# Converting a weight slot's blocks in one instruction per step

## The chip, the cores and the metric

The kernel runs on one core of a Trainium2 chip. The metric is the time of one execution on the device in microseconds (us); the median of several runs is compared. A core has a matrix engine (TensorE, PE in the profile; its weight loads are shown as PEld), a vector engine (VectorE, DVE), a scalar engine for activation functions, copies and casts (ScalarE, ACT), a general one (GpSimd, POOL) and a queue engine (SyncE, SP), which issues all the transfers of this kernel. Each engine works through its own instructions in a fixed order and waits for the others by semaphores.

## The reference

Local and global attention, then two feed-forward layers over the 2304 tokens, 512 wide, in float32:

```python
# attention: 4 batches, 8 heads, 512 local tokens (window +-32) and 32 global ones, head 64
out_g = softmax(q_g @ [k_g, k_l]^T / 8) @ [v_g, v_l]
out_l = softmax([q_l @ k_g^T, masked q_l @ k_l^T] / 8) @ [v_g, v_l]
x = concat(out_g, out_l)                       # 2304 x 512
# layer 1: w_gate, w_val 512 x 1536, w_out 1536 x 512
xn = x / sqrt(mean(x * x) + 1e-6) * rms_g
x = (silu(xn @ w_gate) * (xn @ w_val)) @ w_out
# layer 2: w_in 512 x 2048, w_out 2048 x 512
h = relu(x @ w_in)
out = (s * h * h + b) @ w_out
```

The weights come as float64, as raw 64-bit words.

## The kernel before

**Tiling.** The tokens are split into five groups: three of 512 columns, two of 320. For each group the kernel runs through 28 weight slots: 12 of phase 1 (layer 1, one slot per 128 hidden units: three blocks of 128 x 512, for gate, value and output) and 16 of phase 2 (layer 2: two blocks, input and output). Each float32 product is made of three matmuls with a high and a low part of the operands (`mm3`, lines 584 to 588). A slot's first matmuls go to a PSUM bank (tag `m`, two banks), are turned into `h` on ACT and DVE, and a slot later `emit_second` accumulates `h` times the output block in `acc`. Between the matmuls of a group, `tick` puts in the steps of the attention for the next group and of the build of its `X`, with lags worked out from PE's time.

**Weights.** During group 0 the raw words of the slots come from memory and are converted. `load_raw` (line 146) fetches one block of 512 KB into a tile `wr` (four tiles). `conv(n, j)` (line 156) converts one block: ACT takes the absolute value of the high words (L166), DVE clamps (L167), shifts (L168), puts in the sign (L169) and the low bits (L170, into a tile `wf`), ACT casts to the high part and DVE subtracts for the low part (`hl`, lines 137 to 139). Then the next raw block is asked for, and after a slot's last block the converted slot is written back to memory (`wsc`, L177). The tiles are `cv` (two), `wf` (three) and the weight tiles `w` of three blocks (six, `W_BUFS`). The conversion of slot `n + 2` is emitted in slot `n`, in pieces: after the gate's matmuls, after `h`, after `emit_second`. In groups 1 to 4 `load_w` (line 179) fetches a converted slot, emitted four slots ahead (`W_LEAD`), when a `w` tile is free.

**Start.** `start` (line 450 on) computes the attention of group 0 in eight units (`S_`, `N_`, `T_`, `V_`), builds the first `X` in two halves of 256 columns (`build_steps`: squares, `norm`, `scale`) and converts slots 0 and 1. Its inputs `s_w` lie in four of the six `w` tiles until they are used.

**Order.** The instructions are emitted by the code above and then ordered for each engine, before the run, by a planner that goes by priority and by its own estimate of when operands are ready; `hp(o)` lifts the priority by `o` places. In the run each queue keeps that order. An instruction that finds its tile or its operand not ready holds up all behind it on its engine, on SP too.

Of the kernel before, what the change touches and what calls it, by code (L numbers as in the profile page):

```python
# [9 lines left out]
F32 = mybir.dt.float32  # L10
F32R = mybir.dt.float32r
I32 = mybir.dt.int32
I64 = mybir.dt.int64
AF = mybir.ActivationFunctionType
ALU = mybir.AluOpType
# [36 lines left out]
GN = [sum(seg_len(s) for s in g) for g in GROUPS]  # L52
GO = [sum(GN[:i]) for i in range(len(GN))]
NMAX = max(GN)
W_BUFS = 6
W_LEAD = 4


@with_exitstack
def attn_moe_kernel(ctx: ExitStack, tc: tile.TileContext, s0, q, k, v, w1, w2, cst, out):  # L60
    nc = tc.nc
    pool = lambda name, bufs=1, **kw: ctx.enter_context(tc.tile_pool(name=name, bufs=bufs, **kw))
    cp = pool("cst")
    wr_p = pool("wr", 4)
    cv_p = pool("cv", 2)
    wf_p = pool("wf", 3)
    w_p = pool("w", W_BUFS)
    act_p = pool("act", 2)
    tmp_p = pool("tmp", 2)
# [76 lines left out]
    def load_raw():  # L146
        if nload[0] >= len(blocks):
            return
        n, j = blocks[nload[0]]
        nload[0] += 1  # L150
        ph, _, f = slots[n]
        t = wr_p.tile([128, 512], I64, tag="wr", name="wr")
        nc.sync.dma_start(out=t, in_=(w1 if ph == 1 else w2)[f, :, j])
        wraw[n, j] = t

    def conv(n, j):
        if n >= n0 or j >= nblk(n):
            return
        r = wraw.pop((n, j)).bitcast(I32).rearrange("p (n t) -> p n t", t=2)
        lo, hi = r[:, :, 0], r[:, :, 1]  # L160
        g = cv_p.tile([128, 512], F32, tag="cv", name="cv")
        t = g.bitcast(I32)
        wf = wf_p.tile([128, 512], F32, tag="wf", name="wf")
        w = w_tile(n)
        with hp(20):
            A.activation(out=g, in_=hi.bitcast(F32), func=AF.Abs)  # L166
            V.tensor_scalar(out=g, in0=g, scalar1=W_LO, scalar2=W_HI, op0=ALU.max, op1=ALU.min)  # L167
            V.tensor_scalar(out=t, in0=t, scalar1=3, scalar2=0x3FFFFFFF, op0=ALU.logical_shift_left, op1=ALU.bitwise_and)  # L168
            V.scalar_tensor_tensor(out=t, in0=hi, scalar=-0x40000000, in1=t, op0=ALU.bitwise_and, op1=ALU.bitwise_or)  # L169
            V.scalar_tensor_tensor(out=wf.bitcast(I32), in0=lo, scalar=29, in1=t,  # L170
                                   op0=ALU.logical_shift_right, op1=ALU.bitwise_or)
        with hp(40):
            hl(w[:, j, 0], w[:, j, 1], wf, "A")
        load_raw()
        if j == nblk(n) - 1:
            wsc[n] = dr_p.tile([128, nblk(n), 2, 512], F32, name=f"wsc{n}")
            nc.sync.dma_start(out=wsc[n], in_=w[:, 0:nblk(n)].bitcast(F32))  # L177

    def load_w(n):
        if n < n0 or n >= len(slots):  # L180
# [264 lines left out]
    def start():  # L445
        rw = []
        spare = []

        def ld(i):
            if not spare:  # L450
                t = w_p.tile([128, 2, 1216], F32, tag="w", name="s_w")
                spare.extend((t[:, 0], t[:, 1]))
            t = spare.pop(0)
            nc.sync.dma_start(out=t, in_=s0[i])
            rw.append((t[:, 0:256], t[:, 256:704].rearrange("p (c n) -> p c n", c=2),
                       t[:, 704:1216].rearrange("p (c t h d) -> p c t h d", c=2, t=2, h=2)))

        ld(0)
        nc.sync.dma_start(out=ct, in_=cst)
        ld(1)  # L460
        load_raw()
        ld(2)
        load_raw()
        ld(3)
        load_raw()
        ld(4)
        load_raw()
        for i in (5, 6, 7):
            ld(i)
        A.preload_act_table_set("natural_log_exp_and_others")  # L470
        G.memset(ones, 1.0)
        G.memset(zeros, 0.0)
        G.memset(epsc, EPS)
        G.memset(qf, 0.0)
        G.memset(pg[:, 0:64], 0.0)
        bk = one_bank()
        for _ in range(4):
            PE.matmul(bk[:, 0:128], lhsT=ones, rhs=ones)

        P = [pm[:, 0:2], pm[:, 2:4]]  # L480
        P += [act_p.tile([128, 2, 2, KW], F32, tag="h", name="s_p") for _ in range(2)]
        st = [cp.tile([128, 3, 4], F32, name=f"sst{i}") for i in range(8)]
        bn = [0]

        def nb():
            bn[0] += 1
            return banks("acc0" if bn[0] % 2 else "at")

        def S_(i):
            qr, kr, vr = rw[i]  # L490
            hf, pp = i // 4, P[i % 4]
            bk = nb()
            mms = []
            for c in range(2):
                for h in range(2):
                    x = slice(64 * h, 64 * h + 64)
                    mms.append(PE.matmul(bk[:, h, c * KW:(c + 1) * KW], lhsT=qr[x, 128 * c:128 * c + 128], rhs=kr[x, c]))
            in_turn(mms)
            for h in range(2):
                for c in range(2):  # L500
                    n = 2 * c + h
                    neg_scaled(pp[:, c, h], bk[:, h, c * KW:(c + 1) * KW], cmask(2 * hf + c), st[i][:, 0, n:n + 1])
                for c in range(2):
                    n = 2 * c + h
                    A.activation(out=pp[:, c, h], in_=pp[:, c, h], func=AF.Exp, scale=-1.0,
                                 bias=st[i][:, 0, n:n + 1], accum_out=st[i][:, 1, n:n + 1])

        def N_(i):
            V.tensor_scalar(out=st[i][:, 2], in0=st[i][:, 1], scalar1=1e-9, scalar2=None, op0=ALU.add)
            V.reciprocal(out=st[i][:, 2], in_=st[i][:, 2])  # L510
            for n in range(4):
                x = P[i % 4][:, n // 2, n % 2]
                norm_eng(x, x, st[i][:, 2, n:n + 1], "V")

        pts = {}

        def T_(i):
            bk = nb()
            mms = []
            for c in range(2):  # L520
                for h in range(2):
                    mms.append(PE.transpose(bk[:, c, 256 * h:256 * h + 128], P[i % 4][:, c, h, 0:128], ident))
                    mms.append(PE.transpose(bk[:, c, 256 * h + 128:256 * h + 256], P[i % 4][:, c, h, 96:KW], ident))
            in_turn(mms)
            t = pt_p.tile([128, 2, 2, 2, 128], F32, tag="pt", name="s_pt")
            A.copy(out=t.rearrange("p c h t n -> p c (h t n)"), in_=bk)
            pts[i] = t

        def V_(i):
            bk = one_bank()  # L530
            vr = rw[i][2]
            mms = []
            for c in range(2):
                for ty in (1, 0):
                    for h in range(2):
                        mms.append(PE.matmul(bk[64 * h:64 * h + 64, 128 * c:128 * c + 128], lhsT=vr[:, c, ty, h],
                                             rhs=pts[i][:, c, h, ty], start=(ty == 1), stop=(ty == 0)))
            in_turn(mms)
            o = 2 * (i // 4)
            cpy("A", u_tile(0)[:, i % 4, o:o + 2], bk[:, 0:256].rearrange("p (c n) -> p c n", c=2))  # L540

        bs = [build_steps(0, 0), build_steps(0, 1)]
        S_(0)
        S_(1)
        cb = blocks[:6]
        for i in range(8):
            with hp(100):
                N_(i)
                T_(i)
                if i + 2 < 8:  # L550
                    S_(i + 2)
                V_(i)
            if i < 3:
                conv(*cb[i])
            bs[i // 4][i % 4][0]()
            if i == 3:
                for f in bs[0][4:]:
                    f[0]()
        load_u(0)
        for f in bs[1][4:]:  # L560
            f[0]()
        for i in range(3, 6):
            conv(*cb[i])

    sched = {"q": [], "t": 0.0, "ok": 0.0, "end": 0.0, "x": 0}

# [34 lines left out]
    def emit_second(n, h):  # L601
# [11 lines left out]
        for e in range(4):  # L613
            we = slice(128 * e, 128 * e + 128)
            mm3(acc[e][:, :N], w[:, 0, we], w[:, 1, we], h[:, 0, :N], h[:, 1, :N], f == 0, last)
            if last and ph == 1:
                hl(Y[0][:, 0, e, :N], Y[0][:, 1, e, :N], acc[e][:, :N], "A")
            elif last:
                zt = (wf_p if e % 2 else cv_p).tile([128, NMAX], F32, tag="wf" if e % 2 else "cv", name="z")
                cpy(pick("zz", "AV"), zt[:, :N], acc[e][:, :N])  # L620
                nc.sync.dma_start(out=out[e, :, GO[gi]:GO[gi] + N], in_=zt[:, :N])
            tick()
# [4 lines left out]
    for n, (ph, gi, f) in enumerate(slots):  # L627
# [14 lines left out]
        if ph == 1:  # L642
# [3 lines left out]
            sg = tmp_p.tile([128, NMAX], F32, tag="sg", name="sg")  # L646
            with hp(60):
                A.activation(out=sg[:, :N], in_=gb[:, :N], func=AF.Silu)
            conv(n + 2, 0)
            vb = one_bank()  # L650
            emit_first(vb, w[:, 1], X[gi], N, hs)
            h = act_p.tile([128, 2, NMAX], F32R, tag="h", name="h")
# [1 line left out]
            with hp(60):  # L654
                V.tensor_tensor(out=a[:, :N], in0=sg[:, :N], in1=vb[:, :N], op=ALU.mult)  # L655
                hl(h[:, 0, :N], h[:, 1, :N], a[:, :N], "A")
            conv(n + 2, 1)
            if pend:
                emit_second(*pend.pop())
            pend.append((n, h))  # L660
            conv(n + 2, 2)
        else:
            if f == 0:
                emit_second(*pend.pop())
# [7 lines left out]
            with hp(60):  # L672
# [3 lines left out]
                A.activation(out=h[:, 0, :N], in_=t[:, :N], func=AF.Identity, bias=ct[:, C_B:C_B + 1])  # L676
                V.scalar_tensor_tensor(out=h[:, 1, :N], in0=t[:, :N], scalar=ct[:, C_B:C_B + 1],  # L677
                                       in1=h[:, 0, :N].bitcast(F32), op0=ALU.add, op1=ALU.subtract)
            conv(n + 2, 0)
            if f > 0:  # L680
                emit_second(*pend.pop())
            pend.append((n, h))
            for j in range(1, 3):
                conv(n + 2, j)
    emit_second(*pend.pop())


# [77 lines left out]
```

## Time and profile before

| | |
|---|---|
| median of 3 runs | 1006.13 us (1004.68 to 1007.11) |
| the profiled execution | 1004.7 us |
| its span in the trace | 1002.9 us |
| busy in the span | PE 956.4 us, PEld 808.8, DVE 504.6, ACT 460.1 |
| matmuls | 5608 |
| share of the chain that ended last | PE 82%, DVE 9%, ACT 5%, DMA 3%, issue 1% |
| moved | 243.84 MB, 243 GB/s on the mean |

The span is what the instructions cover; the execution's own time is 1.8 us longer. Matmuls overlap in the records, so a PE that is busy throughout can still be slower than its best. The groups of rows below name the view they come from; idle time in square brackets is what the engine waited just before the instruction, and what ended the wait.

### The profile page before, as it was taken

What the parts mean: (1) busy time and instruction counts of PE and PEld (TensorE: products, weight loads), DVE (VectorE), ACT (ScalarE), POOL (GpSimd) and SP (SyncE); (2) the same over time, 40 slices, a digit from 0 to 9 for tenths busy, and PEclk for the clock granted to TensorE, in tenths of its full rate; (3) what the DMA queues carried; (4) which work ended last, traced back from release to release, by engine and by line L of the source; (5) the groups of instructions that cost most, each with busy time, mean ns of one, the idle gap of its engine ahead of it and who ended that gap; (6) DMA issues with size and microseconds to landing.
All of it is one profiled execution on the core that took longest, in us unless ns stands there. A gap on an engine that the chain in (4) does not pass through costs nothing.

```text
span 1002.9 us, 14529 instructions
## 1 busy us (share of the span) xinstructions
PE 956.4 (95%) x5608; PEld 808.8 (81%) x5608; DVE 504.6 (50%) x1266; ACT 460.1 (46%) x941; POOL 0.8 (0%) x9
## 2 busy tenths in 40 slices
PE   6759999799979999999999999999999999999998
PEld 5548778587858878787877878777889999999997
DVE  6999999999844131434354141443252232421332
ACT  5866495766544162534346262643442342321222
POOL 0000000000000000000000000000000000000000
PEclk9889999999979999999999999999999999999999
DMA  9768979878836553445566544436579748997582
GB/s 371 290 243 282 339 262 381 321 257 320 333 151 223 207 207 141 153 141 209 201 249 245 182 183 146 157 127 227 209 275 335 289 168 293 341 383 269 183 323 108
DMA packets 41109, 243.84 MB, mean 243 GB/s; under 512 B 5072, under 2 KB 6096, under 8 KB 23120
## 3 DMA queue, kind: packets, MB, share of 16 engines
q1 hardware_dynamic: 41040, 242.91, 66.4%
q8 instruction: 44, 0.72, 0.3%
q14 instruction: 25, 0.20, 0.1%
HBM read 202.79 MB, written 40.11 MB: 242 GB/s over the span
## 4 chain that ended last, share of the span: by engine, by line
PE 82%; DVE 9%; ACT 5%; DMA 3%; issue 1%; SPq 0%; ACTq 0%; DVEq 0%
PE m L585 15%; PE m L586 14%; PE m L587 14%; PE acc L585 10%; PE acc L586 10%; PE acc L587 10%; DMA wr<-in_w_dram 2%; PE at L335 2%; PE at L243 2%; ACT pm L266 1%; DVE cv L169 1%; DVE wf L170 1%; DVE wt L139 1%; DVE pm L210 1%; PE at L321 1%
## 5 line engine op out<-in xcount | busy, mean ns | idle before, releaser
L586 PE MATMUL acc<-h,wt 128*128 128x512 f32 (+1 forms) x560 | 200.9, 360 | 0.3 <-DVE h L139 0.3
L587 PE MATMUL acc<-h,wt 128*128 128x512 f32 (+1 forms) x560 | 200.3, 359 | 0.0
L585 PE MATMUL acc<-h,wt 128*128 128x512 f32 (+1 forms) x560 | 190.8, 361 | 1.6 <-DVE y L139 0.9
L585 PE MATMUL m<-x,wt 128*128 128x512 f32 (+2 forms) x496 | 177.1, 358 | 8.2 <-ACT x L133 8.2
L586 PE MATMUL m<-x,wt 128*128 128x512 f32 (+2 forms) x496 | 176.3, 356 | 2.3 <-DVE x L139 2.3
L587 PE MATMUL m<-x,wt 128*128 128x512 f32 (+2 forms) x496 | 175.9, 355 | 0.0
L585 PE MATMUL m<-y,wt 128*128 128x512 f32 (+1 forms) x320 | 116.4, 371 | 10.5 <-DVE t L674 6.9
L586 PEld LDWEIGHTS acc<-h,wt 128*128 128x128 f32 x560 | 105.2, 188 | 14.4 <-DVE h L139 0.7
L586 PE MATMUL m<-y,wt 128*128 128x512 f32 (+1 forms) x320 | 115.9, 362 | 0.8 <-DVE y L139 0.8
L585 PEld LDWEIGHTS acc<-h,wt 128*128 128x128 f32 x560 | 103.6, 188 | 15.9 <-DVE y L139 1.5
L587 PEld LDWEIGHTS acc<-h,wt 128*128 128x128 f32 x560 | 105.2, 188 | 12.9
L587 PE MATMUL m<-y,wt 128*128 128x512 f32 (+1 forms) x320 | 115.4, 361 | 0.0
L655 DVE TENSOR_TENSOR a<-sg,m 128x512 f32<-128x512 f32 (+1 forms) x60 | 36.4, 606 | 151.4 <-PE m L587 137.0
L585 PEld LDWEIGHTS m<-x,wt 128*128 128x128 f32 x496 | 93.8, 190 | 20.8 <-ACT x L133 8.5
L586 PEld LDWEIGHTS m<-x,wt 128*128 128x128 f32 x496 | 93.8, 189 | 14.6 <-DVE x L139 2.8
L587 PEld LDWEIGHTS m<-x,wt 128*128 128x128 f32 x496 | 93.8, 189 | 11.7 <-issue 1.1
L674 DVE SCALAR_TENSOR_TENSOR t<-m,ct,r 128x512 f32<-128x512 f32 (+1 forms) x80 | 53.2, 669 | 92.3 <-ACT r L673 92.0
L673 ACT ACTIVATE r<-m 128x512 f32<-128x512 f32 (+1 forms) x80 | 42.0, 531 | 105.3 <-PE m L587 105.2
L585 PEld LDWEIGHTS m<-y,wt 128*128 128x128 f32 x320 | 59.7, 189 | 23.8 <-ACT y L133 5.5
L676 ACT ACTIVATE h<-t,ct 128x512 fp32r<-128x512 f32 (+1 forms) x80 | 52.3, 658 | 57.6 <-DVE t L674 41.1
L133 ACT CAST h<-a 128x512 fp32r<-128x512 f32 (+1 forms) x60 | 33.2, 554 | 97.6 <-DVE a L655 97.6
L677 DVE SCALAR_TENSOR_TENSOR h<-t,ct,h 128x512 fp32r<-128x512 f32 (+1 forms) x80 | 53.5, 669 | 45.7 <-ACT h L676 45.3
(128 smaller groups left out, 1214.2 us busy)
## 6 DMA issues: line engine op xcount, KB each, us to landing
wt<-wsc SPq DMA_DIRECT2D x48, 1536.0 KB, 7.2
wt<-wsc SPq DMA_DIRECT2D x64, 1024.0 KB, 4.8
wr<-in_w_dram SPq DMA_DIRECT2D x68, 512.0 KB, 5.5
wsc<-wt SPq DMA_DIRECT2D x12, 1536.0 KB, 7.1
wsc<-wt SPq DMA_DIRECT2D x16, 1024.0 KB, 5.6
vr<-in_v_dram SPq DMA_DIRECT2D x16, 512.0 KB, 5.4
fk<-in_k_dram SPq DMA_DIRECT2D x16, 448.0 KB, 5.3
s_w<-in_s_dram SPq DMA_DIRECT2D x8, 608.0 KB, 10.0
```

The lines of the kernel that those rows point to most:

```text
L133: A.copy(out=out_, in_=in_)
L139: V.tensor_tensor(out=dst_l, in0=src, in1=dst_h.bitcast(F32), op=ALU.subtract)
L243: mms.append(PE.matmul(bk[:, h, (c - c0) * KW:(c - c0 + 1) * KW], lhsT=qr[x, o:o + 128], rhs=kr[x, c]))
L335: mms.append(PE.matmul(bk[64 * h:64 * h + 64, 128 * c:128 * c + 128], lhsT=vr[:, c, ty, h], rhs=S["pt", c // 2 * 2][:, c % 2, h, ty], star ...
L585: PE.matmul(out_, lhsT=wh, rhs=xh, start=first, stop=False)
L586: PE.matmul(out_, lhsT=wh, rhs=xl, start=False, stop=False)
L587: PE.matmul(out_, lhsT=wl, rhs=xh, start=False, stop=last)
L655: V.tensor_tensor(out=a[:, :N], in0=sg[:, :N], in1=vb[:, :N], op=ALU.mult)
L673: A.activation(out=r[:, :N], in_=hb[:, :N], func=AF.Relu)
L674: V.scalar_tensor_tensor(out=t[:, :N], in0=hb[:, :N], scalar=ct[:, C_S:C_S + 1], in1=r[:, :N], op0=ALU.mult, op1=ALU.mult)
L676: A.activation(out=h[:, 0, :N], in_=t[:, :N], func=AF.Identity, bias=ct[:, C_B:C_B + 1])
L677: V.scalar_tensor_tensor(out=h[:, 1, :N], in0=t[:, :N], scalar=ct[:, C_B:C_B + 1], in1=h[:, 0, :N].bitcast(F32), op0=ALU.add, op1=ALU.subt ...
```

## The change

A slot's raw blocks lie in one tile of three blocks (`wr`, two tiles instead of four of one block), and `conv` takes a range of blocks. From slot 2 on each step of the conversion is one instruction over all blocks of the slot: 3 x 512 = 1536 columns in phase 1, 2 x 512 = 1024 in phase 2. Slots 0 and 1 are converted block by block as before. `conv(n + 2)` is emitted at one place of slot `n`, after the gate's activation in phase 1 and after `h` in phase 2, instead of at three. The step that puts in the low bits writes in place in `cv`, which has three blocks now; `wf` is gone. The raw blocks of slot `n + 2` are asked for together when slot `n` is converted, ahead of its write-back; at the start six blocks are asked for instead of four. Weight tiles go from six to five, and weight loads are emitted three slots ahead instead of four. Half of the output tiles `z` use the buffers `ta` instead of `wf`.

```diff
-W_BUFS = 6
-W_LEAD = 4
+W_BUFS = 5
+W_LEAD = 3
...
-    wr_p = pool("wr", 4)
+    wr_p = pool("wr", 2)
     cv_p = pool("cv", 2)
-    wf_p = pool("wf", 3)
...
-        t = wr_p.tile([128, 512], I64, tag="wr", name="wr")
-        nc.sync.dma_start(out=t, in_=(w1 if ph == 1 else w2)[f, :, j])
-        wraw[n, j] = t
-
-    def conv(n, j):
-        if n >= n0 or j >= nblk(n):
+        if not j:
+            wraw[n] = wr_p.tile([128, 3, 512], I64, tag="wr", name="wr")
+        nc.sync.dma_start(out=wraw[n][:, j], in_=(w1 if ph == 1 else w2)[f, :, j])
+
+    def conv(n, j0, j1):
+        if n >= n0:
             return
-        r = wraw.pop((n, j)).bitcast(I32).rearrange("p (n t) -> p n t", t=2)
-        lo, hi = r[:, :, 0], r[:, :, 1]
-        g = cv_p.tile([128, 512], F32, tag="cv", name="cv")
+        nb_ = nblk(n)
+        j1 = min(j1, nb_)
+        raw = wraw[n][:, j0:j1]
+        r = raw.bitcast(I32).rearrange("p j (n t) -> p j n t", t=2)
+        lo, hi = r[:, :, :, 0], r[:, :, :, 1]
+        w = w_tile(n)
+        wh, wl = w[:, j0:j1, 0], w[:, j0:j1, 1]
+        gt = cv_p.tile([128, 3, 512], F32, tag="cv", name="cv")
+        g = gt[:, 0:j1 - j0]
         t = g.bitcast(I32)
-        wf = wf_p.tile([128, 512], F32, tag="wf", name="wf")
-        w = w_tile(n)
...
-            V.scalar_tensor_tensor(out=wf.bitcast(I32), in0=lo, scalar=29, in1=t,
-                                   op0=ALU.logical_shift_right, op1=ALU.bitwise_or)
+            V.scalar_tensor_tensor(out=t, in0=lo, scalar=29, in1=t, op0=ALU.logical_shift_right,
+                                   op1=ALU.bitwise_or)
         with hp(40):
-            hl(w[:, j, 0], w[:, j, 1], wf, "A")
-        load_raw()
-        if j == nblk(n) - 1:
-            wsc[n] = dr_p.tile([128, nblk(n), 2, 512], F32, name=f"wsc{n}")
-            nc.sync.dma_start(out=wsc[n], in_=w[:, 0:nblk(n)].bitcast(F32))
+            hl(wh, wl, g, "A")
+        if j1 == nb_:
+            if n + 2 < n0:
+                for _ in range(nblk(n + 2)):
+                    load_raw()
+            wsc[n] = dr_p.tile([128, nb_, 2, 512], F32, name=f"wsc{n}")
+            nc.sync.dma_start(out=wsc[n], in_=w[:, 0:nb_].bitcast(F32))
...
         for i in (5, 6, 7):
             ld(i)
+        load_raw()
+        load_raw()
...
             if i < 3:
-                conv(*cb[i])
+                conv(cb[i][0], cb[i][1], cb[i][1] + 1)
...
-                zt = (wf_p if e % 2 else cv_p).tile([128, NMAX], F32, tag="wf" if e % 2 else "cv", name="z")
+                zt = (tmp_p if e % 2 else cv_p).tile([128, NMAX], F32, tag="ta" if e % 2 else "cv", name="z")
...
-            conv(n + 2, 0)
+            conv(n + 2, 0, 3)
             vb = one_bank()
...
-            conv(n + 2, 1)
             if pend:
                 emit_second(*pend.pop())
             pend.append((n, h))
-            conv(n + 2, 2)
...
-            conv(n + 2, 0)
+            conv(n + 2, 0, 3)
             if f > 0:
                 emit_second(*pend.pop())
             pend.append((n, h))
-            for j in range(1, 3):
-                conv(n + 2, j)
```

## Rows read from the trace of the kernel before

**Rows 1.** Busy time per engine (count), granted clock, DMA share, by stretch.

```profile
80.00:280.00 200.00, 194.48 (x1053) 156.27 (x1054) 188.01 (x421) 130.14 (x246) 0.00 (x0) 1.00 0.86 312
300.00:500.00 200.00, 198.89 (x1095) 160.37 (x1095) 68.11 (x181) 79.42 (x160) 0.00 (x0) 1.00 0.52 186
```

**Rows 2.** Timeline of the start: start, us, engine, line, instruction, [idle before].

```profile
69.44 0.80 PE L585 MATMUL m<-x,wt 128*128 128x256 f32 x2 [8.19 <-ACT x L133]
...
72.14 0.58 PE L586 MATMUL m<-x,wt 128*128 128x256 f32 x1 [1.91 <-DVE x L139]
```

**Rows 3.** Busy time by stretches of 20 us.

```profile
180.00:200.00 20.00, 15.17 (x67) 10.11 (x66) 19.96 (x55) 14.86 (x36) 0.00 (x0) 1.00 0.84 309
...
280.00:300.00 20.00, 13.35 (x71) 9.06 (x69) 9.46 (x21) 8.62 (x17) 0.00 (x0) 0.74 0.41 158
...
500.00:520.00 20.00, 20.00 (x87) 15.32 (x86) 13.15 (x19) 10.97 (x19) 0.00 (x0) 1.00 0.61 223
```

**Rows 4.** Timeline of PE, 184 to 297 us.

```profile
200.67 0.50 PE L585 MATMUL m<-y,wt 128*128 128x512 f32 x1 [1.96 <-DVE t L674]
...
295.25 0.76 PE L585 MATMUL m<-y,wt 128*128 128x512 f32 x1 [3.07 <-DVE t L674]
```

**Rows 5.** Instructions on the weight tiles: count, ns min/median/max, first and last start.

```profile
L133 ACT CAST wt<-wf x68: 602/620/640, 13.1 to 278.5; 128x512 fp32r<-128x512 f32 x68
```

**Rows 6.** Groups by line and shape, 75 to 200 us: busy, mean ns, idle.

```profile
L139 DVE TENSOR_TENSOR wt<-wf,wt 128x512 fp32r<-128x512 f32 x36 | 24.6, 684 | 1.1 <-ACT wt L133 1.1
...
L167 DVE TENSOR_SCALAR cv<-cv 128x512 f32<-128x512 f32 x36 | 15.1, 419 | 1.2 <-ACT cv L166 1.2
...
L217 DVE TENSOR_SCALAR pm<-pm,rs 128x224 f32<-128x224 f32 x4 | 1.1, 333 | 0.0
L139 DVE TENSOR_TENSOR x<-xn,x 128x256 fp32r<-128x256 f32 x2 | 0.8, 413 | 0.0
...
L282 DVE TENSOR_SCALAR pg<-pg,gm 128x544 f32<-128x544 f32 x1 | 0.5, 495 | 0.0
...
L166 ACT ACTIVATE cv<-wr 128x512 f32<-128x512 f32 x36 | 24.3, 674 | 6.5 <-DMA wr<-in_w_dram 6.5
L133 ACT CAST wt<-wf 128x512 fp32r<-128x512 f32 x35 | 21.7, 619 | 17.6 <-DVE wf L170 17.6
...
L133 ACT CAST x<-xn 128x256 fp32r<-128x256 f32 x2 | 0.7, 397 | 0.0
```

**Rows 7.** Timeline of DVE in the start: neighbours of one kind, and dependent ones.

```profile
9.19 0.43 DVE L167 TENSOR_SCALAR cv<-cv 128x512 f32<-128x512 f32 x1 [1.30 <-ACT cv L166]
...
9.65 0.43 DVE L168 TENSOR_SCALAR cv<-cv 128x512 int32<-128x512 int32 x1
...
34.01 0.76 DVE L168 TENSOR_SCALAR cv<-cv 128x512 int32<-128x512 int32 x2
...
34.69 1.29 DVE L169 SCALAR_TENSOR_TENSOR cv<-wr,cv 128x512 int32<-128x512 int32 x2
```

**Rows 8.** Timeline of DVE, 61 to 69 us.

```profile
61.08 0.41 DVE L424 SCALAR_TENSOR_TENSOR nt<-r 128x256 f32<-128x256 f32 x1
61.41 0.68 DVE L169 SCALAR_TENSOR_TENSOR cv<-wr,cv 128x512 int32<-128x512 int32 x1
...
63.59 0.42 DVE L425 TENSOR_TENSOR nt<-nt,msq 128x256 f32<-128x256 f32 x1
...
68.46 0.88 DVE L434 SCALAR_TENSOR_TENSOR xn<-u,ct,r 128x256 f32<-128x256 f32 x2
```

**Rows 9.** Transfers of raw weights: time to landing.

```profile
DMA to landing us min/median/max: 3.4/5.5/11.1
```

**Rows 10.** Who waited for whom, 200 to 290 us: us, times, longest.

```profile
ACT wt L133 <- PE acc L587: 1.6, 3, 0.9
```

**Rows 11.** Relu, 840 to 870 us: count, ns, first and last start.

```profile
L673 ACT ACTIVATE r<-m x9: 437/438/438, 841.1 to 869.3; 128x320 f32<-128x320 f32 x9
```

**Rows 12.** Transfers of converted weights, 826 to 870 us: time to landing.

```profile
DMA to landing us min/median/max: 4.8/6.5/8.8
```

More of the change, by code (lines that the diff above doesn't have):

```diff
@@ L167, in conv @@
             V.tensor_scalar(out=g, in0=g, scalar1=W_LO, scalar2=W_HI, op0=ALU.max, op1=ALU.min)
-            V.tensor_scalar(out=t, in0=t, scalar1=3, scalar2=0x3FFFFFFF, op0=ALU.logical_shift_left, op1=ALU.bitwise_and)
-            V.scalar_tensor_tensor(out=t, in0=hi, scalar=-0x40000000, in1=t, op0=ALU.bitwise_and, op1=ALU.bitwise_or)
-            V.scalar_tensor_tensor(out=wf.bitcast(I32), in0=lo, scalar=29, in1=t,
-                                   op0=ALU.logical_shift_right, op1=ALU.bitwise_or)
-        with hp(40):
-            hl(w[:, j, 0], w[:, j, 1], wf, "A")
-        load_raw()
-        if j == nblk(n) - 1:
-            wsc[n] = dr_p.tile([128, nblk(n), 2, 512], F32, name=f"wsc{n}")
-            nc.sync.dma_start(out=wsc[n], in_=w[:, 0:nblk(n)].bitcast(F32))
+            V.tensor_scalar(out=t, in0=t, scalar1=3, scalar2=0x3FFFFFFF, op0=ALU.logical_shift_left,
+                            op1=ALU.bitwise_and)
+            V.scalar_tensor_tensor(out=t, in0=hi, scalar=-0x40000000, in1=t, op0=ALU.bitwise_and,
+                                   op1=ALU.bitwise_or)
+            V.scalar_tensor_tensor(out=t, in0=lo, scalar=29, in1=t, op0=ALU.logical_shift_right,
+                                   op1=ALU.bitwise_or)
+        with hp(40):
+            hl(wh, wl, g, "A")
[5 more added lines that the diff above has]
+            nc.sync.dma_start(out=wsc[n], in_=w[:, 0:nb_].bitcast(F32))
     def load_w(n):
@@ L562, in start @@
         for i in range(3, 6):
-            conv(*cb[i])
+            conv(cb[i][0], cb[i][1], cb[i][1] + 1)
     sched = {"q": [], "t": 0.0, "ok": 0.0, "end": 0.0, "x": 0}
```

## The prediction

> **What bounds the kernel now.** I read the busy times of the engines by stretch first, then what TensorE (PE) waits for, then the conversion's own instructions. Between 80 and 280 us, where the raw weights are converted beside group 0, PE is busy 194.5 of 200 us and VectorE (DVE) 188.0 [rows 1]: both are nearly full. Between 300 and 500 us, with the same matmul work and no conversion, PE is busy 198.9 and DVE 68.1. So the conversion shares a stage with an engine that is full anyway, and what it costs the end is only what PE stands idle. That idle time lies in three places. At the start, PE waits 8.19 and 1.91 us, 10.1 in all, for the second half of X [rows 2]. At the change from phase 1 to phase 2, the stretch 180 to 200 holds 15.17 us of PE work, so 4.8 are idle [rows 3]; just after it 1.96 us go by for DVE's t [rows 4]. At the end of group 0, the stretch 280 to 300 holds 13.35, so 6.65 are idle, 3.07 of them for t again; the matching stretch of the next group, 500 to 520, is full [rows 3, 4]. No wait of PE for a converted weight shows: the last cast of a weight starts at 278.5 us [rows 5], and the last slot's matmuls still run at 295.25 [rows 4]. The conversion is early; what it does is to stand in front of other DVE work.
>
> **The five DVE steps, merged.** A two-source step over 512 columns takes 684 ns, over 256 columns 413 ns: 1.06 ns a column. A scalar step takes 419 ns at 512; its slope, from 333 ns at 224 and 495 ns at 544 columns, is 0.52 ns [rows 6]. So I estimate 0.684 + 1024 x 0.00106 = 1.77 us for 1536 columns and 1.23 for 1024, and 0.95 and 0.69 for a scalar step. Two independent neighbours overlap: two L169 take 1.29 us, so one starts 0.60 after the other, and two L168 0.76, so 0.34 [rows 7]. A three-block slot now costs DVE 3 x (3 x 0.60 + 2 x 0.34) = 7.44 us, a two-block slot 4.96.
>
> How much merging saves hangs on what stands behind each step. With an unrelated instruction behind it, a merged step costs its duration less the 0.085 (two-source) or 0.08 (scalar) of overlap: 3 x 1.685 + 2 x 0.87 = 6.80, which saves 0.64 per three-block slot, and 3 x 1.14 + 2 x 0.61 = 4.64, which saves 0.32 per two-block slot. Slots 0 and 1 still go block by block, so 10 and 16 slots count: 6.4 + 5.1 = 11.5 us saved. With the slot's own next step behind it, which reads what it wrote, there is no overlap: L168 starts 0.46 us after L167, its 0.43 and 0.03 more [rows 7]. Then the slots cost 3 x 1.80 + 2 x 0.98 = 7.36 and 3 x 1.26 + 2 x 0.72 = 5.22: 0.8 us saved on the ten and 4.2 lost on the sixteen, 3.4 more. The bounds are 11.5 us less and 3.4 more DVE time. Up to five blocks are in flight now (two cv tiles, three wf), two slots then, so both kinds of neighbour will occur; I take 5 us less.
>
> The scalar steps cost half as much per column as the others here, 0.52 against 1.06 ns [rows 6]; that a view of three blocks keeps this no row shows, so the other end is 1.77 instead of 0.95 us, 0.82 x 2 x 10 slots = 16 us more DVE time. The Trainium skill, "Vector Engine (DVE) Microarchitecture Reference", 5.1 Performance modes, ties the doubled rate to an outermost count that is even, or odd and the same on both sides. Three blocks are odd, but both sides are views of one tile; by that rule the rate stays, and the half rate is kept only as a small part of the slow side.
>
> **ScalarE (ACT).** Abs takes 674 ns at 512 columns; a cast 619 at 512 and 397 at 256, 0.87 ns a column [rows 6]. Merged, each takes about 1.5 us. ACT is busy 130 of 200 us [rows 1], so its saving is costed at nothing; what counts is that a Silu, Exp or Relu may find a 1.5 us instruction in front of it instead of 0.67.
>
> **How this reaches PE.** From 80 us on, 5 us less in a DVE that is 94% full lets the attention steps, the y parts and the build of the next X come earlier. What can be regained is the idle time above that a group without conversion doesn't have: 4.8 at the phase change, less about 1 that I leave for its own chain, and 6.65 at the end of the group: 10.4 us. The end's part is a chain of table loads and steps that merging doesn't shorten, only lets begin earlier. I take half, 5 us; bounds 10.4 gained and 4 lost.
>
> At the start the sign turns. The X chain's steps depend on each other, and the queue holds other ready work between them: nt begins at 61.08, its next step only at 63.59, with an L169 (0.60) and more between them; xn comes at 68.46 [rows 8]. For slots 2 to 4 such a filler lasts 1.69 instead of 0.60, 1.1 us more at each place where it stands; but there is one where there were three, and three slots have only 15. Bounds: 2 us gained, if they fall elsewhere, and 8 lost, about seven places of 1.1. I take 1 lost, near the lower end, as the total of DVE work before PE's start hardly changes.
>
> **Loads.** Two raw tiles of a slot hold six or four blocks where four stood. A slot's loads are issued when the conversion of the slot two before it ends, and its Abs waits for all of them. A single block lands in 5.5 us (median; 11.1 at most) [rows 9]; three at once land, by this, in 5.5 to 11. Meanwhile a whole slot is converted, some 7 us of DVE time and more with what stands between. I cost this at nothing: the cover is the lead of the conversion, 278.5 against 295.25. Behind a raw load on SP's queue stand the write-back of weights and the attention's loads; they are late with it, as now.
>
> **One weight buffer less.** In group 0 a cast now waits at times for PE to free a weight tile: 1.6 us in 3 waits after 200 us [rows 10]. With five tiles the conversion stops one slot (5 us of DVE work) sooner, so DVE idles earlier and has more to do in phase 2. This moves work and I cost it at nothing, between 2 gained at the phase change and 4 lost at the end of the group. In the later groups each weight load is issued one slot later. It is tightest in phase 2 of groups 3 and 4: 9 slots start between 841.1 and 869.3, so one per 3.52 us [rows 11]; a load lands in 6.5 us, 8.8 at most [rows 12]. A tile is freed at the end of the slot after its own, so a load has about 2.5 slots, 8.8 us, before its use; now 3.5, 12.3. The cover is 2.3 us at the median and nothing at the worst. I cost it at nothing.
>
> Sum: 5 regained, 1 lost at the start: 4 us. The profiled execution took 1004.7 us (span 1002.9 and 1.8 around it), 1.4 below the median of the runs, 1006.13. 1004.7 - 4 = 1000.7; on the median's scale 1002.
>
> **The rivals.** *Coarse instructions on the start's chain.* The seven places all cost 1.1 us, 8 in all, and only 2 come back later: 1006.1 + 6 = 1012. It decides once the fillers cost over 5 us. For it: DVE is never free for long, and the fillers [rows 8]. Against: there are few of them, and slots 0 and 1 keep the short form. The Trainium skill, "Perfetto Trace Analysis", Optimizing Scalar/DVE Operations, says that grouping pays on a saturated engine, and breaking up where an unsaturated engine makes bubbles on another. Its first half speaks for the forecast between 80 and 280, its second for this rival at the start and at the two seams; the trace has both, so neither half settles it.
>
> *The relief doesn't arrive.* PE is full in most of group 0, the waits at the seams are order in the queues, and gains and losses of 2 us cancel: 1004 to 1008, 1006. For it: PE's 194.5 of 200.
>
> *Weights late in groups 3 and 4.* If loads take over 8.8 us when they overlap, PE waits in some of the 32 slots of phase 2: at 0.5 us each 16 us, 1018 with the gain. For it: the longest landing [rows 12]. Against: the median.
>
> **How the numbers follow.** Forecast 0.42, its own range 995 to 1004. Relief that doesn't arrive 0.22. The slower side 0.36: the start 0.25, late weights 0.06, the half rate and other seams 0.05. About 0.2%, 2 us, is what a measurement can tell from no change: faster 0.42, same 0.22, slower 0.36. The range takes in the start's loss with some of the bounds at the end of the group and leaves out late weights and a full recovery: 994 to 1016.
>
> **What would show it.** Right: merged two-source steps of 1.77 us and scalar steps of 0.95; DVE below 184 of 200 between 80 and 280; under 4 us of PE idle time around 285 to 300; the first long run of matmuls not later than 73 us. Wrong: x's second half later than 75 us (the start), PE waiting for weight loads after 820 us (the buffer), or scalar steps of 1.7 us.

## The result, and the profile after

The changed kernel takes 1015.23 us (median of 4 runs, 1013.31 to 1018.12), the kernel before in the same session 1006.51: a ratio of 1.0094, 95% interval 1.0079 to 1.0108. The change makes the kernel 0.9% slower. 1002 was forecast.

Its profiled execution has a span of 1013.4 us, 10.5 more than before. To see where they arise I took, for each of the 140 slots, the start of its Silu or Relu in both traces. The first Silu comes at 87.0 instead of 81.3 us (+5.7). At the start of group 1 the lag is 4.9, so group 0 with its merged conversion has given back only 0.8. In the first slots of group 1 it rises and settles at 8.0, in those of group 3 at 9.6, late in phase 2 of group 3 at 11.1; it stays there until the last slot (0.6 come back behind it). So there are two large places, the start and the first slots of groups 1 and 3, and a small one.

**The conversion itself** does what was forecast. DVE and ACT groups by line and shape, 85 to 200 us (count, busy, mean ns, idle):

```profile
L138 DVE TENSOR_TENSOR wt<-cv,wt 128x1536 fp32r<-128x1536 f32 x7 | 12.3, 1757 | 4.1 <-ACT wt L132 4.0
L173 DVE SCALAR_TENSOR_TENSOR cv<-wr,cv 128x1024 int32<-128x1024 int32 x6 | 7.3, 1223 | 0.1
L170 DVE TENSOR_SCALAR cv<-cv 128x1536 f32<-128x1536 f32 x5 | 4.8, 955 | 1.7 <-ACT cv L169 1.6
L170 DVE TENSOR_SCALAR cv<-cv 128x1024 f32<-128x1024 f32 x6 | 4.2, 692 | 5.1 <-ACT cv L169 5.1
L132 ACT CAST wt<-cv 128x1536 fp32r<-128x1536 f32 x7 | 10.4, 1481 | 6.0 <-PE acc L596 6.0
L169 ACT ACTIVATE cv<-wr 128x1536 f32<-128x1536 f32 x5 | 8.1, 1612 | 2.6 <-DMA wr<-in_w_dram 2.6
```

Two-source steps take 1757 and 1223 ns, scalar steps 955 and 692: the estimates of 1.77, 1.23, 0.95 and 0.69 from [rows 6] hold. From 512 to 1536 columns a scalar step grows by 536 ns, 0.52 ns a column, so a view of three blocks keeps its rate.

**The stretches** that answer to [rows 1] and [rows 3], and the start (busy time of PE, PEld, DVE, ACT and POOL with counts, granted clock, DMA share, GB/s). First after:

```profile
80.00:280.00 200.00, 196.72 (x1065) 158.72 (x1065) 170.18 (x268) 120.50 (x185) 0.00 (x0) 0.99 0.77 277
180.00:200.00 20.00, 19.98 (x120) 15.46 (x119) 16.76 (x30) 12.27 (x19) 0.00 (x0) 1.00 0.78 277
280.00:300.00 20.00, 11.81 (x78) 8.79 (x77) 9.71 (x17) 9.39 (x11) 0.00 (x0) 0.87 0.71 269
20.00:60.00 40.00, 29.14 (x260) 21.48 (x256) 39.90 (x123) 33.61 (x81) 0.00 (x0) 1.00 0.84 331
60.00:80.00 20.00, 5.73 (x23) 4.83 (x24) 19.96 (x40) 13.66 (x31) 0.00 (x0) 0.57 0.83 319
```

and the last two stretches of the kernel before:

```profile
20.00:60.00 40.00, 32.98 (x257) 24.56 (x254) 38.98 (x138) 33.18 (x87) 0.00 (x0) 0.91 0.72 264
60.00:80.00 20.00, 8.90 (x51) 7.72 (x49) 18.67 (x55) 14.27 (x37) 0.00 (x0) 0.74 0.79 284
```

Between 80 and 280 us DVE falls from 188.0 to 170.2 of 200, below the 184 that the prediction named. At the start it goes the other way: from 20 to 80 us DVE is busy 59.86 of 60 us, where it was 57.65. Part of the relief is thus not saved but moved: conversion that now lies ahead of 80 us.

**The seams of group 0.** PE's waits from the first to the last slot of group 0 (us in total, times, longest), first before:

```profile
PE m L585 <- DVE t L674: 5.0, 2, 3.1
PE at L417 <- DVE ss L410: 2.1, 1, 2.1
PE at L243 <- DVE msq L423: 1.5, 1, 1.5
PE m L585 <- ACT y L133: 1.1, 1, 1.1
PE acc L585 <- DVE y L139: 0.9, 1, 0.9
PE m L586 <- DVE y L139: 0.8, 1, 0.8
```

then after:

```profile
PE m L594 <- DVE t L681: 6.2, 2, 3.3
PE at L424 <- DVE ss L417: 2.3, 1, 2.3
PE at L250 <- DVE msq L430: 1.5, 1, 1.5
```

The two seams go different ways. At the phase change the waits for `y` are gone and the one for `t` is longer, 2.86 us instead of 1.96 [rows 4]. Busy time around it, first before, then after:

```profile
175.00:215.00 40.00, 34.50 (x183) 26.23 (x182) 39.43 (x93) 27.91 (x58) 0.00 (x0) 1.00 0.76 279
```

```profile
175.00:215.00 40.00, 37.12 (x199) 29.43 (x198) 33.81 (x63) 25.21 (x46) 0.00 (x0) 1.00 0.74 255
```

PE is idle 5.5 us there before and 2.9 after. At the end of group 0 nothing is won: the wait for `t` is 3.31 us instead of 3.07, those for `ss` and `msq` are 2.3 and 1.5 instead of 2.1 and 1.5, and one of 1.1 us for `ptf` is new. DVE is busy 184.6 of the 228 us of group 0, where it was 204.8 of 229.

**The start.** PE's waits of the first slots, answering to [rows 2]:

```profile
61.27 0.50 PE L594 MATMUL m<-x,wt 128*128 128x256 f32 x2 [2.22 <-ACT x L132]
65.31 0.58 PE L595 MATMUL m<-x,wt 128*128 128x256 f32 x1 [3.54 <-DVE x L138]
76.83 0.80 PE L594 MATMUL m<-x,wt 128*128 128x256 f32 x2 [9.02 <-ACT x L132]
```

The wait of 8.19 us became 9.02 and ends 7.4 us later, at 76.83 instead of 69.44; the two waits for X's first half are new, and the 1.91 us behind it shrank to 0.44. Its reason stands in DVE's queue; the chain of X's second half with what lies between (timeline of DVE, after; start, us):

```profile
65.51 0.41 DVE L430 TENSOR_SCALAR msq<-acc 128x256 f32<-128x256 f32 x1
...
65.91 1.75 DVE L173 SCALAR_TENSOR_TENSOR cv<-wr,cv 128x1536 int32<-128x1536 int32 x1
67.58 0.42 DVE L431 SCALAR_TENSOR_TENSOR nt<-r 128x256 f32<-128x256 f32 x1
...
69.17 1.75 DVE L175 SCALAR_TENSOR_TENSOR cv<-wr,cv 128x1536 int32<-128x1536 int32 x1
70.84 0.42 DVE L432 TENSOR_TENSOR nt<-nt,msq 128x256 f32<-128x256 f32 x1
...
74.19 1.75 DVE L138 TENSOR_TENSOR wt<-cv,wt 128x1536 fp32r<-128x1536 f32 x1
75.86 0.87 DVE L441 SCALAR_TENSOR_TENSOR xn<-u,ct,r 128x256 f32<-128x256 f32 x2
```

This looks like the first rival: 1.75 us fillers between the links of a chain. The experiments show that it isn't.

**The first slots of group 1.** DVE's waits from 320 to 360 us, then its timeline and PE's, then SP's issues (SP's columns: start, us of issuing):

```profile
DVE a L664 <- DMA out_dram<-z: 9.5, 1, 9.5
```

```profile
335.98 0.69 DVE L664 TENSOR_TENSOR a<-sg,m 128x512 f32<-128x512 f32 x1 [9.48 <-DMA out_dram<-z]
```

```profile
336.72 0.50 PE L594 MATMUL m<-x,wt 128*128 128x512 f32 x1 [1.42 <-DVE a L664]
```

```profile
325.74 0.33 SPq L189 DMA_DIRECT2D wt<-wsc  x1
326.17 1.13 SPq L630 DMA_DIRECT2D out_dram<-z  x2
```

`a` needs a `ta` buffer, and an output tile `z` is still in it. Its transfer is issued 0.43 us behind a weight load of 1.5 MB, and `a` starts 9.8 us after that issue. With `wf` under `z`, nobody waited there. From 750 to 800 us the same wait is 7.8 us in 2.

**The small place.** Between 860 and 875 us PE waits once for a weight load:

```profile
PE m L594 <- DMA wt<-wsc: 0.9, 1, 0.9
```

### The profile page after: what moved, and what is told of

The parts are those of the page before. It is cut to its first block, busy times and chain, and to the rows that moved or that the text cites. A ratio compares the mean times of both kernels' runs of the same rounds, so it can differ in the third digit from the quotient of the medians.

```text
span 1013.4 us, 14228 instructions
## 1 busy us (share of the span) xinstructions
PE 957.1 (94%) x5608; PEld 808.2 (80%) x5608; DVE 492.0 (49%) x1086; ACT 453.0 (45%) x869; POOL 0.8 (0%) x9
## 4 chain that ended last, share of the span: by engine, by line
PE 81%; DVE 10%; DMA 4%; ACT 3%; issue 1%; SPq 0%; DVEq 0%; ACTq 0%
PE m L594 15%; PE m L595 14%; PE m L596 14%; PE acc L594 10%; PE acc L595 10%; PE acc L596 10%; PE at L342 2%; DMA out_dram<-z 2%; PE at L250 2%; DMA wt<-wsc 1%; DVE pm L217 1%; DVE cv L173 1%; DVE cv L175 1%; DVE wt L138 1%; PE at L328 1%
## 5 line engine op out<-in xcount | busy, mean ns | idle before, releaser
L594 PEld LDWEIGHTS m<-x,wt 128*128 128x128 f32 x496 | 93.7, 190 | 28.5 <-ACT x L132 11.9
L596 PEld LDWEIGHTS m<-x,wt 128*128 128x128 f32 x496 | 94.2, 190 | 11.5 <-issue 0.8
```

What stands on the lines that cost most here:

```text
L594: PE.matmul(out_, lhsT=wh, rhs=xh, start=first, stop=False)
L596: PE.matmul(out_, lhsT=wl, rhs=xh, start=False, stop=last)
```

## The experiments

The theory: two separate losses, the start and `z` in `ta`, and a small one from late weights. For the start the rivals were the long fillers, the five weight tiles and the loads. Each ratio is against the kernel before in the same session.

**`z` out of `ta`.**

```diff
+    z_p = pool("z", 2)
...
-                zt = (tmp_p if e % 2 else cv_p).tile([128, NMAX], F32, tag="ta" if e % 2 else "cv", name="z")
+                zt = (z_p if e % 2 else cv_p).tile([128, NMAX], F32, tag="z" if e % 2 else "cv", name="z")
```

> The changed kernel with one thing different: the half of the output tiles z that it puts into the two buffers `ta` gets two buffers of its own. Theory (the step `a` of phase 1 has to wait until an output tile's transfer has left a `ta` buffer): the two steps in the difference of the traces, 3.1 us in slots 3 to 5 of group 1 and 1.6 us in slots 2 to 5 of group 3, go away, 4.7 us in all, so about 1010.5 us; the start stays at 87 us for the first Silu. Rival (the transfers of that stretch are late for everything, and `a` only happens to be where it shows): PE waits for the next weights instead, 1014 to 1015 us.

Measured: 1010.48 us, ratio 1.0027 (1.0016 to 1.0038). That is 4.7 us less by the medians of the two sessions, 6.7 by the ratios, 5.9 between the two traces; the small place is in these numbers, as it goes too. The first Silu stays at 87.0; the lag holds at 5.2 to 5.3 us from slot 4 of group 1 to the last slot, so the steps at groups 1 and 3 are gone, and the small one behind them too. DVE's waits from 320 to 360 us no longer hold a transfer:

```profile
DVE a L665 <- PE m L597: 19.1, 3, 6.7
DVE z L135 <- PE acc L597: 5.9, 1, 5.9
```

The theory holds, and the rival (weights just as late) falls.

**`z` in `ta`, in the kernel before.** The edit is that of the change's `z` line alone.

```diff
-                zt = (wf_p if e % 2 else cv_p).tile([128, NMAX], F32, tag="wf" if e % 2 else "cv", name="z")
+                zt = (tmp_p if e % 2 else cv_p).tile([128, NMAX], F32, tag="ta" if e % 2 else "cv", name="z")
```

> The kernel before with one thing different: half of its output tiles z go into the `ta` buffers, as in the change. Theory (the wait of `a` for the output transfer is a cost of that edit alone): 4.7 us slower than before, about 1011 us, in the first slots of groups 1 and 3. Rival (it costs only when the weight loads are issued a slot later, as in the change): 1006 to 1007 us, no difference.

Measured: 1008.05 us, ratio 1.0019 (1.0004 to 1.0035): 1 to 2 us, less than the 4.7 expected. From 740 to 800 us `a` waits for a transfer of `z`:

```profile
DVE a L655 <- DMA out_dram<-z: 7.4, 1, 7.4
```

From 320 to 360 us the profile puts a wait of the same length down to PE. The transfer's own times show that it is `z` there too (SP's issue of two tiles, their time to landing, and DVE):

```profile
324.11 0.86 SPq L621 DMA_DIRECT2D out_dram<-z  x2
DMA to landing us min/median/max: 7.6/7.7/7.8
331.85 0.69 DVE L655 TENSOR_TENSOR a<-sg,m 128x512 f32<-128x512 f32 x1 [7.41 <-PE at L322]
```

The first tile lands at 331.72, 7.6 us after its issue, and `a`, which waits for the semaphore of that transfer, starts 0.13 us later; a PE instruction happened to end at the same time. Each of the two waits raises the lag by 1.4 us, 2.8 in all, against 3.1 and 1.6 in the change. So the theory holds in kind, as the wait comes with that edit alone and in both places, and the rival falls. The price is lower here, with a wait of 7.4 us in group 1 against 9.5; why is not shown.

**Five weight tiles, in the kernel before.**

```diff
-W_BUFS = 6
-W_LEAD = 4
+W_BUFS = 5
+W_LEAD = 3
```

> The kernel before with five weight tiles instead of six and weight loads emitted three slots ahead instead of four. Theory (the buffer costs only what the late weights of groups 3 and 4 showed): 1 to 1.5 us slower, about 1007.5 us, all of it after 700 us; first Silu at 81.3 us as before. Rival (the start's inputs hold four of five tiles, so the start is late through the buffer and not through the merging): first Silu at 85 to 87 us, 1011 to 1013 us in all.

Measured: 1005.67 us, ratio 0.9985 (0.9974 to 0.9995). Neither the start's loss nor one after 700 us is in it; the lag in its trace is 1.0 us from slot 4 of group 1 on and doesn't grow. The buffer costs nothing here; the kernel is, if anything, 0.5 to 2.6 in a thousand faster, and both sides of the expectation were too high.

**One instruction per block again.** Tiles, loads and the place of emission stay those of the change.

```diff
-        raw = wraw[n][:, j0:j1]
-        r = raw.bitcast(I32).rearrange("p j (n t) -> p j n t", t=2)
...
+        for j in range(j0, j1):
+            conv_block(n, j, w, gt[:, j - j0])
...
+    def conv_block(n, j, w, g):
+        r = wraw[n][:, j].bitcast(I32).rearrange("p (n t) -> p n t", t=2)
```

`conv_block` holds the seven steps, over the 512 columns of one block.

> The changed kernel with its tiles, its loads, its single place for the conversion and its in-place step, but each step of the conversion as one instruction per block of 512 columns again. Theory (the 1.75 us fillers hold up the chain of the first X): the first Silu is back at about 81 to 82 us and the total at 1009 to 1010 us, the rest of the loss (z, late weights) stays. Rival (the place of emission, six blocks asked for up front, or the buffers are what delays the start): first Silu stays at 86 to 88 us, total 1015 us or more, as DVE has up to 11 us more to do in group 0.

Measured: 1017.5 us, ratio 1.0108 (1.0088 to 1.0129). The first Silu comes at 93.7 us, 6.7 later than merged; PE's longest wait at the start:

```profile
82.53 0.80 PE L596 MATMUL m<-x,wt 128*128 128x256 f32 x2 [13.46 <-ACT x L132]
```

With fillers a third as long the start is worse. So their length isn't the cause, and my theory of the start fell; of the rival's two figures the total came, but the first Silu did not stay. What differs between the traces is how much conversion DVE has done when X comes. I counted it in each timeline: DVE's time up to the first subtraction of X's second half, each instruction charged until the next one starts.

| kernel | X's second half, us | conversion ahead of it | other work | idle | first Silu |
|---|---|---|---|---|---|
| before | 71.7 | 31.9 | 29.5 | 10.3 | 81.3 |
| after | 79.3 | 40.5 | 30.2 | 8.7 | 87.0 |
| after, by blocks | 85.0 | 46.8 | 30.1 | 8.1 | 93.7 |

Other work and idle time are alike, 39 us; the conversion ahead makes the difference. Counted in steps over one block of 512 columns, 64, 87 and 96 lie ahead of X: what the run by blocks adds to the change is mostly more steps, not longer ones, and why it takes in nine more with the same tiles is not shown. The new theory: the change gives the conversion more room. Before, two tiles `cv` and three `wf` of one block limited what was in flight; now two tiles `cv` of three blocks hold six blocks, and the planner's order fills DVE's openings with conversion earlier than the slots need it.

**One conversion tile, in the changed kernel.**

```diff
-    cv_p = pool("cv", 2)
+    cv_p = pool("cv", 1)
```

> The changed kernel with one conversion tile `cv` of a slot instead of two, so that only one slot is converted at a time; the instructions stay as merged. In the run with one instruction per block the first Silu came at 93.7 us, later still than the 87.0 of the change, so long fillers are not the cause of the late start. Theory now (room for six blocks in `cv`, where before two in `cv` and three in `wf` were in flight, lets the order put more conversion ahead of the first X, 44 us of DVE work against 36): with one tile at most one slot runs ahead, the first Silu comes at 78 us or earlier. The rest of group 0 pays, as a slot's chain of seven steps of 1 to 1.8 us, 10 us, no longer overlaps with the next one's: the total is 1010 to 1025 us. Rival (it is the loads, six blocks asked for at once): first Silu stays at 86 to 88 us.

Measured: 1029.79 us, ratio 1.0227 (1.0206 to 1.0248). X's second half comes at 64.2 with 23.0 us of conversion ahead, the first Silu at 69.7, 17.3 us sooner than in the change, with merged instructions and the same loads: 45 steps lie ahead of X instead of 87. So room for conversion moves the start. The rest of group 0 pays more than expected, 262.5 us against 228.8: the chain of one slot no longer overlaps with the next. Waits from 80 to 300 us:

```profile
ACT cv L169 <- DVE wt L138: 19.2, 16, 2.5
...
DVE cv L170 <- ACT cv L169: 15.1, 15, 1.8
DVE wt L138 <- ACT wt L132: 14.1, 13, 2.9
```

**Three tiles `cv`, in the kernel before.**

```diff
-    cv_p = pool("cv", 2)
+    cv_p = pool("cv", 3)
```

> The kernel before with three tiles `cv` of one block instead of two, and nothing else. Theory (room in flight lets conversion run ahead of the first X): DVE has some 5 to 6 us more conversion done when the second half of X comes, first Silu at 85 to 88 us instead of 81.3, total 1009 to 1013 us. Rival (the start of the change is late through merging, loads or five weight tiles): no difference, first Silu at 81 to 82 us, 1006 to 1007 us.

Measured: 1012.89 us, ratio 1.0058 (1.0036 to 1.0080). 35.4 us of conversion lie ahead of X, 3.5 more than before; X's second half comes at 73.6, the first Silu at 84.9 and group 1 5.9 us late. One block more of room, and nothing else, makes the first Silu of the kernel before 3.6 us late (in traces with an untouched start it spreads from 81.3 to 83.0); the other 2.3 us arise within group 0, where the change lost nothing. The conversion moved ahead is less than the 5 to 6 us expected, the total is within the expectation.

**Conversion behind X.** In the changed kernel, and then likewise in the kernel before, an order on ACT: Abs of slot 3 and later slots comes after the last of the eight casts of the first X, which are kept in the list `xc`.

```diff
-            A.activation(out=g, in_=hi.bitcast(F32), func=AF.Abs)
+            ab = A.activation(out=g, in_=hi.bitcast(F32), func=AF.Abs)
+            if n >= 3 and len(xc) == 8:
+                tc.add_manual_dep(ab.ins, xc[7].ins.name, behind, reason="after x")
```

> The changed kernel with an order put on ACT: the first step (Abs) of the conversion of slot 3 and of all later slots comes behind the last cast of the first X. Theory (conversion work in front of X is the start's loss): 17 us of DVE work move behind X, first Silu at 72 to 78 us; if the conversion then keeps ahead of the slots, the gain reaches group 1 in part, total 1004 to 1011 us. Rival (the chain of attention steps sets the start, and conversion only fills its gaps): first Silu not before 81 us, total 1010 to 1016 us.

> The kernel before with the same order on ACT: the first conversion step of slot 3 and later slots comes behind the last cast of the first X. Theory: 12 us of DVE work move behind X, PE's waits of 8.19 and 1.91 us ahead of the first full slot shrink, first Silu at 72 to 77 us, total 998 to 1005 us if the end of group 0 doesn't take it back. Rival (the attention's chain sets the start, or DVE, 94 per cent busy until 280 us, gives the gain back at the end of group 0): 1005 to 1010 us.

Measured: 1000.79 us for the changed kernel, ratio 0.9939 (0.9915 to 0.9963), and 1000.53 for the kernel before, 0.9943 (0.9922 to 0.9964). X's second half comes at 62.6 and 65.3 us with 22.0 and 22.9 us of conversion ahead; the first Silu at 70.8 and 71.6. PE's wait for it, first in the changed kernel, then in the kernel before:

```profile
62.55 0.80 PE L597 MATMUL m<-x,wt 128*128 128x256 f32 x2 [4.32 <-ACT x L132]
```

```profile
65.18 0.50 PE L588 MATMUL m<-x,wt 128*128 128x256 f32 x2 [4.22 <-ACT x L133]
```

The theory holds at the start in both and the rivals fall; the first Silu comes slightly sooner than expected, and the changed kernel's total is 3 us below its 1004 to 1011. In the changed kernel 16.2 us won at the start are 12.6 at group 1 (303.2 against 315.8), so 3.6 are given back in group 0; in the kernel before 9.7 become 5.4. Both then beat the kernel before as it was; the changed one still pays its `z`.

**Both mendings together, and what slot 2 is worth.** The order above with `z` in its own buffers; and the same with the conversion of slot 2 behind X too, where the condition is

```diff
-            if n >= 3 and len(xc) == 8:
+            if n >= 2 and len(xc) == 8:
```

> The changed kernel with both mendings: the first conversion step of slot 3 and later slots behind the last cast of the first X, and two buffers of their own for the half of the output tiles that went into `ta`. Theory (two separate losses): the 14 us of the first and the 4.7 us of the second add up, 995 to 997 us. Rival (the second is hidden behind the first, since weight loads and output transfers then stand differently): 1000 to 1001 us.

> As the run with both mendings, but slot 2's conversion stands behind the first X too. Theory (what stands in front of X is what counts): 5 us less DVE work in front, first Silu at 66 to 69 us instead of about 71, total 993 to 996 us. Rival (from here the attention's chain sets the start, and slot 2's weights come late): first Silu at 70 to 71 us, PE waits for slot 2's casts, 996 to 1000 us.

Measured: 997.71 us, ratio 0.9907 (0.9893 to 0.9921), and 998.09, ratio 0.9911 (0.9896 to 0.9926). The first total is just above the 995 to 997 expected, the second in the rival's range. The mendings add up, though `z` is worth 3.1 us here and not 4.7. Slot 2 brings the first Silu from 71.0 to 68.6 us with 15.2 us of conversion ahead, but no time: between these two no difference can be measured. DVE's idle time ahead of X has gone from 11.0 to 15.2, so less work in front no longer moves X one for one. The first of the two is 9 us faster than the kernel before.

**Merging by itself.** As the first run with both mendings, with the edit of the run by blocks:

```diff
+        for j in range(j0, j1):
+            conv_block(n, j, w, gt[:, j - j0])
```

> As the run with both mendings, but each conversion step is one instruction per block of 512 columns again. It prices merging by itself, in a kernel whose start and output tiles are in order. Theory (merging saves DVE 11.5 us at most, which reaches the end only at the seams of group 0): 2 to 5 us slower than the merged form, first Silu within 1 us of it. Rival (merging is worth nothing, as PE is full in group 0): within 1 us of it. Second rival (short instructions let the chains of X and of the attention through sooner): 1 to 4 us faster.

Measured: 1003.21 us, ratio 0.9957 (0.9941 to 0.9973): merging is worth 5.5 us. Busy time from 80 to 280 us, first merged, then by blocks:

```profile
80.00:280.00 200.00, 193.56 (x1030) 153.32 (x1029) 179.09 (x271) 124.18 (x186) 0.00 (x0) 0.99 0.86 321
```

```profile
80.00:280.00 200.00, 193.02 (x1018) 154.01 (x1018) 190.49 (x429) 129.21 (x246) 0.00 (x0) 0.99 0.85 316
```

DVE has 11.4 us less to do, but of this only 1.3 us reach the end within group 0: the lag between the two is 4.0 us at the first Silu (71.0 against 75.0) and 5.3 at group 1 (304.2 against 309.5). What merging visibly shortens in group 0 is PE's wait for `y` at the phase change, first merged, then by blocks (from 80 to 310 us):

```profile
PE m L598 <- ACT y L133: 1.0, 1, 1.0
```

```profile
PE m L600 <- ACT y L133: 4.0, 2, 3.8
```

The other 4.0 us lie ahead of the first Silu, where I had expected the two within 1 us; the total of 5.5 is just above the 2 to 5 expected. They hardly come from more work on DVE. In both kernels 45 steps over one block lie ahead of X, and X's first half comes at 52.2 and 52.4 us. Then DVE takes up a step of the attention, `pm`, first merged, then by blocks:

```profile
54.17 0.38 DVE L220 CUSTOM_DVE_ANT_0 pm<-at,ct 128x224 f32<-128x224 f32 x1
```

```profile
58.61 0.39 DVE L222 CUSTOM_DVE_ANT_0 pm<-at,ct 128x224 f32<-128x224 f32 x1 [3.71 <-PE at L255]
```

By blocks it waits 3.71 us for PE, with X's second half behind it in the queue; the wait for `r` that follows is 1.46 us by blocks and 2.39 merged, so DVE idles about 3 us longer ahead of X. These 3 of the 5.5 us are a difference of the two orders; that merging must bring it about is not shown.

The Trainium skill, "Perfetto Trace Analysis", Optimizing Scalar/DVE Operations, says that grouping can improve throughput on a saturated engine and that breaking up may help where an unsaturated engine makes bubbles on another. The first pair agrees with the first half: DVE is busy 59.86 of 60 us at the start of the change, PE waits for it, and the short instructions moved the first Silu from 87.0 to 93.7 us. In the second pair DVE is not full from 20 to 80 us, busy 55.6 us merged and 53.8 by blocks, and the short instructions didn't help there either.

## Why the prediction failed

**The durations, the rate and the buffer were right.** The merged durations stand above. DVE's saving was taken as 5 us out of bounds of 11.5 less and 3.4 more; 11.4 were measured between the two kernels that differ by merging alone. Of the 130 merged steps in the trace of the change, 100 are overlapped by the next instruction, 11 are followed without overlap, and behind 19 DVE idles. (The scalar slope of 0.52 ns a column is 162 / 320 = 0.51 by the two rows it was read from; the measured step bears out 0.52.) The half rate didn't come: 955 ns for 1536 columns. This agrees with what the Trainium skill, "Vector Engine (DVE) Microarchitecture Reference", 5.1 Performance modes, says of an odd count that is the same on both sides. One weight buffer less was costed at nothing, and measured as 0.9985.

**"Half of the seams' 10.4 us comes back" failed, by its larger part.** Group 0 took 229.6 us from its first Silu to group 1's before and 228.8 after: 0.8 us, not 5. In the two pairs that differ by merging alone it is 1.3 and about 0. The smaller part came: at the phase change PE is idle 2.9 us instead of 5.5. The end of the group, 6.65 us of the 10.4, gave nothing back; its four waits are 8.2 us together, where three were 6.7. The prediction set that idle time against a group without conversion and gave DVE's load the blame. But PE's waits for `t`, `ss` and `msq` are as long with a DVE that is busy 184.6 of 228 us as with one busy 204.8 of 229: so they are no queue that a lighter DVE empties; the likeliest reading, not shown by itself, is the length of the chain of dependent steps. Why the same seam is full in later groups was not tried.

**"The total of DVE work before PE's start hardly changes" failed,** and with it the size of the start's loss, 5.7 us at the first Silu instead of 1. The conversion ahead of X grew by 8.6 us, 31.9 to 40.5, and X's second half came 7.6 us later, at 79.3, past the 75 that the prediction had named as a sign. The prediction looked at what each instruction costs between two links of the chain and not at how many of them the order would place there. The runs with one and with three tiles `cv` show that the buffers move that number. The prediction had counted them ("up to five blocks are in flight now", "two slots then"), but used the count only to judge which neighbours overlap. The 5.7 us lost at the first Silu lie within the bound of 8, and the first rival with its 1012 us is nearest to what came; but it came to that by the length of the fillers, and shorter ones were 6.7 us worse. Its condition was met by another mechanism.

**A term was missing.** Half of the output tiles move into `ta`; the change was described and never costed. It is worth 4.7 us by the medians, the late weights with it, from an `a` that waits for a transfer. Every tile that moves needs the name of who takes that buffer next.

**Weights late** showed as one wait of 0.9 us and a step of 1.5 us in the lag, in the change alone; with `z` in its own buffers it is gone. That a `z` transfer caused it is not shown. The forecast of 1002 lacked the start (5.7 instead of 1), `z` (4.7 instead of 0) and the seams (0.8 instead of 5): 1002 + 4.7 + 4.7 + 4.2 = 1015.6. That it comes so close is in part luck, as `z` is worth 4.7 to 6.7 by the way it is taken. The measured 1015.2 is within the range, near its upper end, on the side that had 0.36.

Open: which part of the room matters, the `cv` tiles alone or also the raw tiles with six blocks asked for at once, was tested for `cv` only; the single place of emission was not run apart.

## What to carry to other kernels

More buffers for a side job can cost time: an order that fills an engine's openings with whatever is ready will put more of that job ahead of the chain that the end waits for, so count the side job's work in front of the chain, not only the length of one filler, and if needed put it behind by an explicit order. What merging saves on a full engine, 11.4 us here, reaches the end only where the path waits for that engine; idle time that stays the same with a lighter engine is not to be regained so. A tile that an output transfer still reads is taken until the transfer lands, so its buffers should not be those of a step on the path. And a wait that the profile puts down to an engine can be a transfer's: compare its end with the landings.

## What the runs showed that was not expected

An output tile's transfer can take as long as a weight load: the two loads of 1.5 MB issued from 318 to 338 us after take 8.8 us in the median. The transfers of `z` from 320 to 360 us after, time to landing:

```profile
DMA to landing us min/median/max: 2.0/5.9/9.7
```

The longest is five times the shortest. And the start varies between traces: with the same conversion ahead of X (31.9 to 32.0 us), the first Silu came at 81.3 (before), 82.8 (`z` in `ta`) and 83.0 us (five tiles), so steps of under 2 us there can't be read from one trace.
